# Attention and Fourier-mix feed-forward on one core: the first feed-forward group in its written order, with the last batch's folds and transform moved up

## The chip, the cores and the metric

The kernel runs on one core of a Trainium2 chip. The time is that of one execution on the device, in microseconds (us). Engines are called as in the profile: PE (TensorE, matrix products), PEld (its weight loads), DVE (VectorE), ACT (ScalarE), POOL (GpSimd) and SP (SyncE, which here only issues DMAs). Each works through its own instructions in order, and semaphores make one wait for another.

## What is computed

Attention with a window of 128 and 4 sink tokens, for 4 batches of 768 tokens and 8 heads of 64; then a layer that mixes by a two-dimensional Fourier transform and a feed-forward network with a ReLU, all in 32-bit floats:

```python
keep = is_sink | in_window
scores = np.where(keep, scale * q @ k.T, -1e9)
a = softmax(scores)
x = (a @ v)                                  # 4 x 768 x 512, heads side by side
mixed = np.real(np.fft.fft(np.fft.fft(x, axis=1), axis=2))
u = x + mixed
un = (u - mean(u)) / np.sqrt(var(u) + 1e-6)
out = u + np.maximum(un @ w_ch1, 0.0) @ w_ch2    # 512 -> 2048 -> 512
```

## The kernel before

**Precision.** Each operand of a large product is split into a high part, rounded to PE's fast 32-bit format, and a low part, the difference. A product is then three products: high by high, high by low, low by high. So most tiles have a copy on ACT that makes the high part (L365 `fold_hi`, L402 `z_hi`, L610 and L624 in `convert`) and a subtraction on DVE or POOL that makes the low part (L368 `fold_lo`, L410 `z_lo`, L611, L625).

**Stages.** The attention runs in steps `s`, four to a block of 128 tokens and 24 blocks over all batches. The order of each engine's operations within a step is a hand-written table (`SCHEDULE`), and each operation lags behind the scores by a fixed number of steps. `store_x` (L862) writes a block's result to `u`. A batch's transform (`fourier`, L333) is woven into the steps after it as events: `at(s, engine, fn)` puts a function on a step, and `run_ev` issues it when that step comes. Its parts are

- folds: `fold_n` (L352, sum and difference of block `j` and its mirror block `j + 3`), `fold_m` (L359, L362), `fold_hi`, `fold_lo`, for `j` of 0 to 2. `ready[j]` is the step at which block `j` has been stored, and the folds lie `F_N`, `F_M`, `F_S` steps behind it: 3, 4 or 5, 6 or 7.
- `stage1` (L395): five products (`za` twice, `zr`, `zb` twice), one a step for the last batch, the first of them `S1 = 7` steps behind `ready[2]`. Each has its `z_hi` on ACT and `z_lo` on DVE one step later.
- `stage2a` (L422) and `stage2b` (L443), then `combine` (L448, L449), and `update` (L459, L460), which adds to the rows of `u` and for batches not kept on the chip stores them to DRAM (L462, tile `ud`).

The transform's products take turns on two PSUM banks, and a product waits until the one before it in its bank has been read.

**Feed-forward groups.** The 3072 tokens make six groups of 512. Group 0 (from L1251) takes the hidden layer in 16 turns `f`: `ch1` (L656, 12 matmuls: a block of 128 hidden units), `split` (L1146 ReLU on ACT, L1147 low part on DVE) and `ch2` of the turn before (L1154, 12 matmuls). During these turns the weights arrive. `load_w` fetches a raw block (L584), and `convert(i)` turns it from pairs of 32-bit words into high and low parts, with three DVE passes (L599, L600, L601), a copy on ACT and a subtraction on POOL. Turn `f` converts numbers `2f+4` and `2f+5`; numbers 0 and 1 are events of attention steps 100 and 102, and 2 and 3 stand ahead of turn 0. The blocks of the first matrix go through `w_ring`, whose space the attention's keys held before. For every two of them, `combine_w1` makes sums on POOL (L636 to L639), and a turn later ACT and POOL make high and low parts of these (L643, L644); both are stored to DRAM (L614, L645) for the groups that follow. Block 7 of the second matrix and the later ones go into a pool that is opened when the last batch's transform has finished and its space is free (L1270, L1271).

Events that are left when the attention ends are issued by `do(1)`, one or two steps to a turn, until all are flushed in turn 5.

From turn 6 on (`PREP`), three steps of `prepare(1)` stand at the end of each turn (`PREP_N`). They make the normalized input of group 1: statistics (L515, L516), small operations for the deviations (L522 to L531), normalization (L539), a transposition on PE (L545) with ACT's copy (L1199), sums (L1227 to L1233) and the high and low parts of these (L1237, L1238). Groups 1 to 5 run in a loop of products with the combined weights (L1320) and the second matrix (L1348).

**What sets the order.** Inside `tc.manual_schedule()` each engine's instructions stay in the order in which the program writes them. Outside, the framework's scheduler orders them by its own estimates. In the kernel before, attention steps 0 to 96 (`CUT = 97`) and the loop from L1304 are inside. Steps 97 to 109, and group 0 with the rest of the last transform, are the scheduler's.

Of the kernel before, what the change touches and what calls it, by code (L numbers as in the profile page):

```python
# [11 lines left out]
F32 = mybir.dt.float32  # L12
# [7 lines left out]
P = 128  # L20
# [39 lines left out]
FOLD_AT, FOLD_LAST, FOLD_ENG = (0, 4, 8), (0, 4, 8), "VG"  # L60

F_N, F_M, F_S, ROW = (3, 3), (4, 5), (6, 7), (5, 8, 10)
EV_A = 0

SINK0_AT = 3, 3, "V"
# [71 lines left out]
EV_D, EV_Z = 1, 1  # L137
X_AT, X_NOT = (2,), (81, 97)
SOFT_AT = (0, 1, 2, 3)
S1, S2, UD = 7, 1, 2  # L140
FFT_ORDER = (2, 1, 0)
PARTS = {0: ((2,) * 5, 1, 1), 1: ((2,) * 5, 2, 1), 2: ((2,) * 5, 2, 1)}
PARTS_TAIL = ((1,) * 5, 1, 1)
# [61 lines left out]
def kernel(  # L205
# [17 lines left out]
    def f32(ap):  # L223
        return ap.bitcast(F32)
# [46 lines left out]
    def run(general):  # L271
        tag = "g" if general else ""
        with ExitStack() as p1:
# [8 lines left out]
            def at(s, eng, fn):  # L282
                ev.setdefault((s, eng), []).append(fn)
# [49 lines left out]
            def fourier(b, at, ready):  # L333
# [15 lines left out]
                def fold_n(eng, j, odd):  # L349
                    t = fw.tile([P, DM], F32, tag=f"f{odd}", name=f"f{odd}_{b}_{j}", bufs=2 - odd)  # L350
                    t_["eo", j, odd] = t
                    eng.tensor_tensor(t, u[j], u[NHALF + j], op=ALU.subtract if odd else ALU.add)  # L352

                def fold_m(eng, j, odd):

                    g = t_["eo", j, 0]
                    if odd:
                        t = t_.pop(("eo", j, odd))
                        eng.tensor_tensor(g[:, 257:512], t[:, 1:256], t[:, 511:256:-1], op=ALU.subtract)  # L359
                        t_["g", j] = t_.pop(("eo", j, 0))  # L360
                    else:
                        eng.tensor_tensor(g[:, 1:256], g[:, 1:256], g[:, 511:256:-1], op=ALU.add)  # L362

                def fold_hi(j):
                    A.copy(gh[:, j], t_["g", j])  # L365

                def fold_lo(j):
                    V.tensor_tensor(gl[:, j], t_.pop(("g", j)), f32(gh[:, j]), op=ALU.subtract)  # L368
# [97 lines left out]
                for j in range(NHALF):  # L466
                    k = ready[j]
                    e0, e1 = FOLD_TAIL if tail else FOLD_ENG
                    eng = {"V": V, "G": G}
                    at(k + F_N[0], e0, lambda j=j: fold_n(eng[e0], j, 0))  # L470
                    at(k + F_N[1], e1, lambda j=j: fold_n(eng[e1], j, 1))
                    at(k + F_M[0], e0, lambda j=j: fold_m(eng[e0], j, 0))
                    at(k + F_M[1], e1, lambda j=j: fold_m(eng[e1], j, 1))
                    at(k + F_S[0], "A", lambda j=j: fold_hi(j))
# [155 lines left out]
            def combine_w1(p, pool):  # L630

                t = state.pop(("t", p))
                b11, b21, b12, b22 = t[:, 0, :256], t[:, 0, 256:], t[:, 1, :256], t[:, 1, 256:]
                q = pool.tile([P, 4, 256], F32, tag="tq", name=f"tq{p}")
                o = pool.tile([P, 4, 2, 256], F32R, tag="to", name=f"to{p}")
                G.tensor_tensor(q[:, 1], b12, b11, op=ALU.subtract)  # L636
                G.tensor_tensor(q[:, 0], b22, q[:, 1], op=ALU.subtract)  # L637
                G.tensor_tensor(q[:, 2], b22, b12, op=ALU.subtract)
                G.tensor_tensor(q[:, 3], b21, q[:, 0], op=ALU.subtract)  # L639

                def halves():
# [503 lines left out]
            def split(h, x):  # L1145
                A.activation(h[0], x, AF.Relu)  # L1146
                V.scalar_tensor_tensor(h[1], x, 0.0, f32(h[0]), op0=ALU.max, op1=ALU.subtract)  # L1147
# [100 lines left out]
                        run_ev(s, e)  # L1248
                    s += 1

            po = [ps_o.tile([P, DM], F32, tag=f"o{i}", name=f"o{i}_0") for i in range(len(groups[0]))]  # L1251
            hs = {}
            for i in (2, 3):
                convert(i, wa)
            combine_w1(0, g0)
            for f in range(NF):
                ps = hp.pop(0) if f < 2 else ch1(0, f, unT0)
                hs[f] = [g0.tile([P, 512], F32R, tag=f"h{i}", name=f"h{i}_{f}", bufs=2) for i in range(2)]
                split(hs[f], ps)
                if pw is None:  # L1260
                    do(1)
                if f > 0:
                    ch2(f - 1, hs.pop(f - 1), po)
                for i in range(2 * f + 4, min(2 * f + 6, 2 * NF)):
                    if i % 2 and pw is None:
                        do(1)
                    if W_ORDER[i][0] == 1 and W_ORDER[i][1] == NWA + NHALF and pw is None:
                        while ev:
                            do(1)
                        pf.close()  # L1270
                        pw = p1.enter_context(tc.tile_pool(name="wb" + tag, bufs=1))  # L1271
                        state["x"] = [pw.tile([P, 7, 512], F32R, name=f"x{i}") for i in range(2)]
                        state["xf"] = pw.tile([P, 2, NCC, 256], F32, name="xf")
                    convert(i, wa if pw is None else pw)
                while late:
                    late.pop()()
                if f % 2 == 1 and f // 2 + 1 < NPR:
                    combine_w1(f // 2 + 1, g0)
                if f == PREP:
                    steps = prepare(1)  # L1280
                for _ in range(PREP_N if f >= PREP else 0):
                    next(steps, None)
            for _ in steps:
                pass
            while late:
                late.pop()()

            places = [npool.tile([P, 2, 2, 256], F32R, tag="ld", name=f"w1_c{i}", bufs=LDB) for i in range(LDB)]
            n_all = (len(groups) - 1) * NIT * 7

            def load(n):
                if n < n_all:
                    it, k = divmod(n % (NIT * 7), 7)
                    for j in range(2):
                        nc.sync.dma_start(f32(places[n % NWS][:, j]).rearrange("p s c -> p (s c)"), w_dram[2 * it + j][:, W_PLACE[k]])

            for n in range(LDB):
                load(n)
            ch2(NF - 1, hs.pop(NF - 1), po)
            for i in range(len(po)):  # L1300
                finish(0, i, po[i])
# [187 lines left out]
```

## Time and profile before

| | us |
|---|---|
| Median of three runs (774.32 to 775.8) | 774.68 |
| The profiled execution | 772.87 |
| Its span | 771.1 |
| PE busy | 731.0 |
| DVE busy | 531.6 |
| POOL busy | 291.5 |
| ACT busy | 266.5 |

The granted PE clock was 0.992 on average. The page's second part divides the span into 40 slices of 19.3 us and gives the busy share of each in tenths. In the lists of instructions, columns are start, duration, engine and line, operation, tiles written and read, shapes and count; in brackets stands the idle time of the engine ahead of the instruction and what ended it. In groups, the numbers behind the bar are the busy time and the mean duration in ns, and then the idle time ahead with what ended it. "PE L656" is `ch1`, "PE L1154" `ch2`, "PE L1320" the first product of the loop of groups 1 to 5. Matmuls overlap, so that a unit of 12 shows 2.9 us and the next starts earlier than that.

### The profile page before, as it was taken

The page shows a single profiled execution, that of the slowest core. Times are in us where ns is not written, and L with a number is a line of the kernel's source. Part 1 is how long each engine was busy: PE and PEld are TensorE (multiplying, and loading weights), DVE is VectorE, ACT ScalarE, POOL GpSimd, SP SyncE. Part 2 cuts the span into 40 slices and gives each one's busy share as a digit, 9 for nine tenths or more (in the row PEclk, how much of TensorE's full clock was granted, in tenths as well). Part 3 has the DMA queues.
Part 4 walks back from the last instruction along what each step waited for, and adds up shares of the span by engine and source line. Part 5 has one row for each costly group of instructions (what it writes and reads, how often), then busy time and mean ns, then how long its engine had stood idle before and what let it go on. Part 6 is the DMA issues. An engine that isn't in the chain of part 4 may idle for free.

```text
span 771.1 us, 13868 instructions
## 1 busy us (share of the span) xinstructions
PE 731.0 (95%) x4899; PEld 624.4 (81%) x4899; DVE 531.6 (69%) x1411; ACT 266.5 (35%) x743; POOL 291.5 (38%) x387
## 2 busy tenths in 40 slices
PE   8999998979879898989999999999999999999996
PEld 6676876757668686868989998998998998898895
DVE  6878578899689887867783677467764778342323
ACT  4787666656632324421103111221122110311110
POOL 2567477478779679650015000520034001500000
PEclk9999999999998999999999999999999999999999
DMA  9763525644404678879655756567555655565601
GB/s 307 255 167 114 154 84 169 195 128 139 164 1 191 229 258 282 281 246 378 218 183 180 256 193 191 177 216 254 171 168 189 218 176 183 183 222 170 190 28 60
DMA packets 84446, 145.90 MB, mean 189 GB/s; under 512 B 7532, under 2 KB 32236, under 8 KB 82960
## 3 DMA queue, kind: packets, MB, share of 16 engines
q1 hardware_dynamic: 84080, 141.17, 56.5%
q0 software_dynamic: 288, 3.76, 1.2%
q8 instruction: 41, 0.67, 0.4%
q14 instruction: 37, 0.30, 0.1%
HBM read 120.77 MB, written 24.13 MB: 188 GB/s over the span
## 4 chain that ended last, share of the span: by engine, by line
PE 54%; POOL 2%; DVE 2%; DMA 2%; issue 1%; ACT 1%; SPq 0%; POOLq 0%; DVEq 0%; ACTq 0%
PE o L1348 29%; PE pB L1320 11%; PE pC L1320 7%; PE pA L1320 7%; DMA wd<-to 1%; POOL to L644 1%; DMA w_b<-wd 1%; PE o L1154 0%; DVE u L1159 0%; DVE x L1238 0%; POOL w_ring L611 0%; PE h L656 0%; POOL w L625 0%; POOL tq L639 0%; POOL tq L637 0%
## 5 line engine op out<-in xcount | busy, mean ns | idle before, releaser
L1348 PE MATMUL o<-w,hring 128*128 128x512 f32 x780 | 192.1, 392 | 0.0
L1348 PEld LDWEIGHTS o<-w,hring 128*128 128x128 f32 x780 | 142.4, 188 | 28.2
L1146 ACT ACTIVATE hring<-tmp 128x512 fp32r<-128x512 f32 x60 | 37.9, 632 | 174.8 <-DVE tmp L1393 84.6
L1227 POOL TENSOR_TENSOR s<-xf 128x512 f32<-128x512 f32 x4 | 5.2, 1294 | 240.3 <-DVE xf L1206 240.3
L1147 DVE SCALAR_TENSOR_TENSOR hring<-tmp,hring 128x512 fp32r<-128x512 f32 x60 | 51.8, 863 | 45.6 <-ACT hring L1146 45.6
L1206 DVE STREAM_TRANSPOSE xf<-un 32x128 f32<-32x128 f32 x256 | 77.4, 302 | 3.5
L764 ACT ACTIVATE sm<-sm,mx 128x132 f32<-128x132 f32 x192 | 75.9, 400 | 3.9 <-DVE mx L758 3.9
L1320 PE MATMUL pB<-x,w_b 128*128 128x256 f32 x456 | 59.4, 279 | 0.8 <-DMA w_b<-wd 0.8
L1320 PEld LDWEIGHTS pB<-x,w_b 128*128 128x128 f32 x456 | 56.6, 188 | 1.8 <-issue 1.0
L739 PE MATMUL s<-ring,q 64*128 64x260 f32 x320 | 49.2, 411 | 8.3 <-DVE mx L758 4.3
L758 DVE CUSTOM_DVE_ANT_0 sm<-s,mask 128x132 f32<-128x132 f32 x192 | 48.4, 292 | 8.0 <-PE s L737 3.2
L1147 DVE SCALAR_TENSOR_TENSOR hring<-pA,hring 128x512 fp32r<-128x512 f32 x20 | 13.8, 691 | 57.0 <-ACT hring L1146 57.0
L656 PE MATMUL h<-un_slots,w_ring 128*128 128x512 f32 x192 | 48.6, 400 | 1.5 <-ACT w_ring L610 0.9
L1146 ACT ACTIVATE hring<-pA 128x512 fp32r<-128x512 f32 x20 | 11.9, 596 | 100.2 <-PE pA L1320 100.2
L739 PEld LDWEIGHTS s<-ring,q 64*128 64x128 f32 x320 | 26.8, 185 | 21.0 <-DVE mx L758 5.3
L656 PEld LDWEIGHTS h<-un_slots,w_ring 128*128 128x128 f32 x192 | 35.7, 190 | 9.6 <-ACT w_ring L610 1.3
L1348 PE MATMUL o<-w_gh,hring 128*128 128x512 f32 x120 | 42.5, 395 | 0.0
L834 PE MATMUL xt<-ptl,ldv 128*64 128x128 f32 x384 | 38.8, 285 | 3.1 <-POOL ptl L812 3.1
L1154 PE MATMUL o<-w,h 128*128 128x512 f32 x156 | 39.3, 400 | 1.3 <-POOL w L625 0.8
L1320 PEld LDWEIGHTS pC<-x,w_b 128*128 128x128 f32 x288 | 36.9, 188 | 2.0
L1320 PE MATMUL pA<-x,w_b 128*128 128x256 f32 x288 | 37.5, 279 | 0.5 <-DMA w_b<-wd 0.5
L803 ACT COPY pta<-pt 128x512 f32<-128x512 f32 x48 | 28.1, 584 | 28.5 <-PE pt L796 28.5
(222 smaller groups left out, 1559.6 us busy)
## 6 DMA issues: line engine op xcount, KB each, us to landing
w_b<-wd SPq DMA_DIRECT2D x172, 256.0 KB, 3.5
w_c<-wd SPq DMA_DIRECT2D x108, 256.0 KB, 3.5
raw<-in_moe_w_ch_dram SPq DMA_DIRECT2D x32, 512.0 KB, 4.7
wd<-to SPq DMA_DIRECT2D x8, 1024.0 KB, 6.7
ldv<-in_v_dram SPq DMA_DIRECT2D x28, 256.0 KB, 3.3
ring<-in_qk_dram SPq DMA_DIRECT2D x24, 264.0 KB, 5.0
wd<-w_ring SPq DMA_DIRECT2D x8, 768.0 KB, 3.9
out_dram<-u SPq DMA_DIRECT2D x24, 256.0 KB, 2.5
```

The lines of the kernel that those rows point to most:

```text
L656: T.matmul(ps[:, :tb], a[cc], x[:, :, cc, :], start=n == 0, stop=n == 3 * NCC - 1)
L739: T.matmul(ps[:, j, :P + W], st["q", g][rows, hp, :], keys(g, 2 * hp + j), start=True, stop=True)
L758: V.tensor_tensor_reduce(sm[:, h % 4], ps[:, j, P:P + W], mask[min(qi, 3)], -SCALE, 3.0e38, ALU.add, ALU.min, accum_out=mx[:, 0, h:h + 1])
L764: A.activation(sm[:, h % 4], sm[:, h % 4], AF.Exp, bias=mx[:, 0, h:h + 1], scale=-1.0, accum_out=mx[:, 1, h:h + 1])
L803: A.copy(a, st.pop(("pt", g, hp // 2)))
L834: T.matmul(ps[D * j:D * j + D, p, :], st["v", kb(g) - i][:, h, :], a[:, h % 4, :], start=i == 0, stop=i == n - 1)
L1146: A.activation(h[0], x, AF.Relu)
L1147: V.scalar_tensor_tensor(h[1], x, 0.0, f32(h[0]), op0=ALU.max, op1=ALU.subtract)
L1154: T.matmul(po[i], a[:, ts_], x, start=f == 0 and n == 0, stop=f == NF - 1 and n == 2)
L1206: V.transpose(place[32 * q:32 * q + 32, :, r], un[r].rearrange("p (c q j) -> p c q j", c=NCC, q=4)[:, :, q])
L1320: T.matmul(ps[:, 256 * j:256 * j + 256], w[:, j, a, cs], x[:, xs], start=BANK.index(BANK[k]) == k and j == c == m == 0, stop=j == c == 1 a ...
L1348: T.matmul(po[i], h[:, a, j, ts_], x, start=first and j == m == 0, stop=last and j == 1 and m == 2)
```

## The change

Group 0 goes inside a manual schedule, from the allocation of its accumulators to the closing of its pool, otherwise unchanged and only indented. For the last batch, the folds of its last block lie 1, 2 and 3 steps behind the block instead of 3 to 7, and the first stage of its transform 4 steps behind instead of 7. As all later events of that transform are counted from there, they come three steps earlier.

```diff
+F_LAST = (1, 1), (2, 2), (3, 3)
...
-S1, S2, UD = 7, 1, 2
+S1, S1_LAST, S2, UD = 7, 4, 1, 2
...
                     eng = {"V": V, "G": G}
-                    at(k + F_N[0], e0, lambda j=j: fold_n(eng[e0], j, 0))
-                    at(k + F_N[1], e1, lambda j=j: fold_n(eng[e1], j, 1))
...
-                    at(k + F_S[1], "V", lambda j=j: fold_lo(j))
+                    f_n, f_m, f_s = F_LAST if tail and j == NHALF - 1 else (F_N, F_M, F_S)
+                    at(k + f_n[0], e0, lambda j=j: fold_n(eng[e0], j, 0))
+                    at(k + f_n[1], e1, lambda j=j: fold_n(eng[e1], j, 1))
...
+                    at(k + f_s[1], "V", lambda j=j: fold_lo(j))
...
-                k = ready[2] + S1
+                k = ready[2] + (S1_LAST if tail else S1)
...
-            po = [ps_o.tile([P, DM], F32, tag=f"o{i}", name=f"o{i}_0") for i in range(len(groups[0]))]
-            hs = {}
-            for i in (2, 3):
-                convert(i, wa)
-            combine_w1(0, g0)
-            for f in range(NF):
...
-            pg.close()
+            with tc.manual_schedule():
+                po = [ps_o.tile([P, DM], F32, tag=f"o{i}", name=f"o{i}_0") for i in range(len(groups[0]))]
+                hs = {}
+                for i in (2, 3):
+                    convert(i, wa)
+                combine_w1(0, g0)
+                for f in range(NF):
...
+                pg.close()
```

More of the change, by code (lines that the diff above doesn't have):

```diff
@@ L469, in fourier @@
                     eng = {"V": V, "G": G}
-                    at(k + F_N[0], e0, lambda j=j: fold_n(eng[e0], j, 0))
-                    at(k + F_N[1], e1, lambda j=j: fold_n(eng[e1], j, 1))
-                    at(k + F_M[0], e0, lambda j=j: fold_m(eng[e0], j, 0))
-                    at(k + F_M[1], e1, lambda j=j: fold_m(eng[e1], j, 1))
-                    at(k + F_S[0], "A", lambda j=j: fold_hi(j))
-                    at(k + F_S[1], "V", lambda j=j: fold_lo(j))
+                    f_n, f_m, f_s = F_LAST if tail and j == NHALF - 1 else (F_N, F_M, F_S)
+                    at(k + f_n[0], e0, lambda j=j: fold_n(eng[e0], j, 0))
+                    at(k + f_n[1], e1, lambda j=j: fold_n(eng[e1], j, 1))
+                    at(k + f_m[0], e0, lambda j=j: fold_m(eng[e0], j, 0))
+                    at(k + f_m[1], e1, lambda j=j: fold_m(eng[e1], j, 1))
+                    at(k + f_s[0], "A", lambda j=j: fold_hi(j))
+                    at(k + f_s[1], "V", lambda j=j: fold_lo(j))
                 at(ready[0] + ROW[0], "V", put_row)
@@ L1249, in do @@
                     s += 1
-            po = [ps_o.tile([P, DM], F32, tag=f"o{i}", name=f"o{i}_0") for i in range(len(groups[0]))]
-            hs = {}
-            for i in (2, 3):
-                convert(i, wa)
-            combine_w1(0, g0)
-            for f in range(NF):
[L1257 to L1265, printed above, removed]
+            with tc.manual_schedule():
[5 more added lines that the diff above has]
+                for f in range(NF):
+                    ps = hp.pop(0) if f < 2 else ch1(0, f, unT0)
+                    hs[f] = [g0.tile([P, 512], F32R, tag=f"h{i}", name=f"h{i}_{f}", bufs=2) for i in range(2)]
+                    split(hs[f], ps)
+                    if pw is None:
@@ L1266, in run @@
                         do(1)
-                    if W_ORDER[i][0] == 1 and W_ORDER[i][1] == NWA + NHALF and pw is None:
-                        while ev:
+                    if f > 0:
+                        ch2(f - 1, hs.pop(f - 1), po)
+                    for i in range(2 * f + 4, min(2 * f + 6, 2 * NF)):
+                        if i % 2 and pw is None:
                             do(1)
[L1270 to L1273, printed above, removed]
@@ L1274, in run @@
-                    convert(i, wa if pw is None else pw)
+                        if W_ORDER[i][0] == 1 and W_ORDER[i][1] == NWA + NHALF and pw is None:
+                            while ev:
+                                do(1)
+                            pf.close()
+                            pw = p1.enter_context(tc.tile_pool(name="wb" + tag, bufs=1))
+                            state["x"] = [pw.tile([P, 7, 512], F32R, name=f"x{i}") for i in range(2)]
+                            state["xf"] = pw.tile([P, 2, NCC, 256], F32, name="xf")
@@ L1275, in run @@
+                        convert(i, wa if pw is None else pw)
+                    while late:
+                        late.pop()()
+                    if f % 2 == 1 and f // 2 + 1 < NPR:
+                        combine_w1(f // 2 + 1, g0)
+                    if f == PREP:
+                        steps = prepare(1)
+                    for _ in range(PREP_N if f >= PREP else 0):
+                        next(steps, None)
+                for _ in steps:
+                    pass
                 while late:
@@ L1276, in run @@
                     late.pop()()
[L1277 to L1301, printed above, removed]
@@ L1302, in run, with load @@
-            pg.close()
+                places = [npool.tile([P, 2, 2, 256], F32R, tag="ld", name=f"w1_c{i}", bufs=LDB) for i in range(LDB)]
+                n_all = (len(groups) - 1) * NIT * 7
+                def load(n):
+                    if n < n_all:
+                        it, k = divmod(n % (NIT * 7), 7)
+                        for j in range(2):
+                            nc.sync.dma_start(f32(places[n % NWS][:, j]).rearrange("p s c -> p (s c)"), w_dram[2 * it + j][:, W_PLACE[k]])
@@ L1304, in run @@
+                for n in range(LDB):
+                    load(n)
+                ch2(NF - 1, hs.pop(NF - 1), po)
+                for i in range(len(po)):
+                    finish(0, i, po[i])
+                pg.close()
             with tc.manual_schedule():
```

## The prediction, made before the changed kernel was run

> **What bounds the kernel now.** I read the page first, then the busy times by window, then the engines' instructions in order of time.
>
> ```profile
> span 771.1 us, 13868 instructions
> ...
> PE   8999998979879898989999999999999999999996
> ...
> DVE  6878578899689887867783677467764778342323
> ```
>
> From slice 18 on (347 us) TensorE is full to the end; that is the hand-ordered loop of groups 1 to 5, which the change leaves alone. So the change can only move the time at which that loop begins, and everything below is about that time.
>
> ```profile
> 150.00:160.00 10.00, 10.00 (x102) 7.68 (x98) 9.85 (x36) 7.48 (x31) 7.39 (x13) 1.00 0.37 104
> 160.00:170.00 10.00, 6.67 (x52) 4.75 (x53) 9.69 (x34) 5.72 (x22) 6.57 (x11) 1.00 0.60 194
> ...
> 190.00:200.00 10.00, 10.00 (x88) 8.38 (x86) 8.03 (x32) 6.30 (x24) 5.45 (x10) 1.00 0.41 134
> ```
>
> ```profile
> 230.00:235.00 5.00, 2.45 (x8) 2.43 (x8) 5.00 (x6) 1.39 (x4) 4.92 (x5) 0.50 0.42 179
> ...
> 305.00:310.00 5.00, 5.00 (x17) 3.95 (x16) 5.00 (x6) 2.72 (x5) 3.75 (x3) 0.66 0.99 278
> ```
>
> The columns are the stretch and its length, the busy times of PE, PEld, DVE, ACT and POOL, the granted clock, and the DMA share and rate. In 160 to 170 DVE is full and PE is not: attention waits for DVE there, in 190 to 200 it doesn't. Later PE loses time twice over, to waits and to a lower clock after them.
>
> ```profile
> 207.44 0.43 PE L834 MATMUL xt<-ptl,ldv 128*64 128x128 f32 x2 [3.07 <-POOL ptl L812]
> ...
> 219.89 2.94 PE L656 MATMUL h<-un_slots,w_ring 128*128 128x512 f32 x12
> ...
> 232.55 1.01 PE L395 MATMUL za<-cst,gh 128*128 128x386 f32 x2 [5.43 <-ACT asb L431]
> ...
> 236.50 3.06 PE L1154 MATMUL o<-w,h 128*128 128x512 f32 x12
> ...
> 255.22 0.63 PE L395 MATMUL zb<-cst,gh 128*128 128x386 f32 x2 [2.29 <-DVE zr L407]
> ...
> 282.82 2.92 PE L656 MATMUL h<-un_slots,w_ring 128*128 128x512 f32 x12
> ```
>
> ```profile
> 291.14 2.93 PE L1154 MATMUL o<-w,h 128*128 128x512 f32 x12
> 293.90 2.93 PE L656 MATMUL h<-un_slots,w_ring 128*128 128x512 f32 x12
> 296.67 2.93 PE L1154 MATMUL o<-w,h 128*128 128x512 f32 x12
> ...
> 304.19 0.66 PE L545 MATMUL unt<-ident,un 128*128 128x128 f32 x4 [2.75 <-ACT xf L1199]
> ...
> 344.80 1.58 PE L1320 MATMUL pA<-x,w_c 128*128 128x256 f32 x12
> ```
>
> A unit of 12 matmuls takes 2.77 us (291.14 to 293.90 to 296.67), a turn of the group's loop over f (ch1 and ch2) 5.53. The unit of ch1(7) starts at 282.82 and the loop of group 1 at 344.80. I call 207.44 to 282.82 the first half and the 62.0 us after it the second.
>
> **The change part by part.** The three runs have a median of 774.68 us; the profiled execution took 772.87 (span 771.1), 1.8 less. The sum below is a difference made against the profiled one, and I put it on the median.
>
> *1. Conversions leave the attention.* Where no hand order holds, the scheduler has pulled weight conversions forward:
>
> ```profile
> 154.29 1.17 DVE L599 TENSOR_SCALAR tw<-raw 128x512 int32<-128x512 int32 x1
> ...
> 162.61 0.41 DVE L599 TENSOR_SCALAR tw<-raw 128x512 int32<-128x512 int32 x1
> ```
>
> ```profile
> L599 DVE TENSOR_SCALAR cv<-raw x6: 410/424/1485, 182.2 to 251.3; 128x512 int32<-128x512 int32 x6
> ```
>
> ```profile
> 200.93 5.88 POOL L611 TENSOR_TENSOR w_ring<-tw,w_ring 128x512 fp32r<-128x512 f32 x4
> 206.76 0.63 POOL L812 TENSOR_SCALAR_AFFINE_SELECT ptl<-pta 128x512 f32<-128x512 f32 x1
> ```
>
> Only conversions 0 and 1 are issued in the attention's own steps. In a written group, number 2 and later come behind the attention's hand order. The two at 154.29 and 162.61 stood where DVE was the limit: with two more passes of 0.69 each (rows in step 3) 4.3 us. The `cv` ones from 182.2 on stood where PE was full. I take -3.0 (0 to -4.4), nearer to the row of 160 to 170. On POOL four low passes, 1.47 each, stand ahead of the mask pass for which PE waits 3.07. Two of them go behind it: -2.9. If the scheduler puts other passes in their place, it is anything up to +3.
>
> *2. Folds and transform, first half.* The last fold now follows the last store by one step, not three.
>
> ```profile
> 220.13 0.68 DVE L862 TENSOR_TENSOR us<-x,mx 128x512 f32<-128x512 f32 x1
> ...
> 234.42 1.22 DVE L368 TENSOR_TENSOR gl<-f,gh 128x512 fp32r<-128x512 f32 x1
> ```
>
> ```profile
> L1147 DVE SCALAR_TENSOR_TENSOR h<-h,h 128x512 fp32r<-128x512 f32 x16 | 10.9, 684 | 8.6 <-ACT h L1146 6.8 <-POOL w L625 1.8
> ...
> L352 DVE TENSOR_TENSOR f<-us,us 128x512 f32<-128x512 f32 x6 | 5.6, 956 | 0.1
> ```
>
> From the store to the end of the low half took 15.5 us, and its own five passes and one cast need some 4. The waits of 5.43 and 2.29 go, and with the first the half clock: 232.55 to 236.50 is 3.95 us at a granted 0.50, so 2.0 of it. Together -9.7. Late next is the second transform product. It needs a PSUM bank that the last combine of batch 2 frees, and this is written behind conversions 2 and 3 (0.41 and twice 0.69, 1.8 each) and split 0 with its ReLU (1.3), 5.6 us with itself; the first product covers 1.7: +3.9. The later low halves, written behind conversions: some +2. Net -3.8 (-9.7 if nothing is late next; +3 if DVE's passes there are drawn out as L352's mean is).
>
> *3. Second half.* Bare, PE needs 19 units and four transpositions, 54.1 of its 62.0 us. In the written order DVE has in each turn one split (0.6 to 0.68) and two conversions:
>
> ```profile
> 282.17 0.69 DVE L599 TENSOR_SCALAR cw<-raw 128x512 int32<-128x512 int32 x1
> 282.89 0.69 DVE L600 SCALAR_TENSOR_TENSOR cw<-raw,cw 128x512 int32<-128x512 int32 x1
> 283.62 0.69 DVE L601 SCALAR_TENSOR_TENSOR tw<-raw,cw 128x512 int32<-128x512 int32 x1
> 284.35 0.69 DVE L599 TENSOR_SCALAR cw<-raw 128x512 int32<-128x512 int32 x1
> ```
>
> They start 2.18 apart, so 4.96 of a turn's 5.53 us are taken and 0.57 are spare. Turns 6 to 13 add the preparation of group 1, three steps a turn. The scheduler had spread it out: statistics at 243.76 and the first normalization at 266.85, long before turn 6.
>
> ```profile
> 243.76 0.67 DVE L515 BATCH_NORM_STATS2 bn<-u 128x6 f32<-128x512 f32 x1
> ...
> 266.85 1.47 DVE L539 TENSOR_SCALAR un<-u,stat 128x512 f32<-128x512 f32 x1
> ...
> 311.33 0.54 DVE L539 TENSOR_SCALAR un<-u,stat 128x512 f32<-128x512 f32 x1
> ```
>
> ```profile
> L1238 DVE TENSOR_TENSOR x<-s,x 128x512 fp32r<-128x512 f32 x4 | 3.0, 762 | 0.7 <-ACT x L1237 0.7
> ...
> L527 DVE SCALAR_TENSOR_TENSOR stat<-stat 128x4 f32<-128x4 f32 x4 | 0.7, 164 | 0.1
> ```
>
> Four statistics of 0.67, 14 small ones of 0.16, four normalizations of 0.54, seven low halves of 0.76 and four sums of the same size make 15.5 us. Eight turns spare 4.6, so DVE falls behind PE by 10.9, and PE, which needs every split and every weight, waits for it. Besides, PE meets DVE at the end of turns 9 and 10: a transposition is written after ch2, and its input on DVE after both conversions. PE is there 2.77 us after ch1 ends; DVE after ReLU 0.6, split 0.68, 4.36 and 0.54, 6.2 in all. With the hand-over through ACT's copy, written behind the casts, 3.9 each time and 7.8 for two, in which DVE has no new ch1 to split. Last, the second matrix's block 7 goes into space that the transform gives back only when its six rows are stored:
>
> ```profile
> 276.91 5.14 SPq L462 DMA_DIRECT2D ud<-us  x6
> ```
>
> Written, ReLU 6 stands behind that block's cast on ACT's queue: 5.14 of issues and a landing (3.5, as a load in step 5), less the turn that covers it, 3.1. Sum 21.8: the half becomes 75.9, +13.9. Bounds: DVE alone has 56 us for 10 splits, 16 conversions and the 15.5, so -6 at best; with its passes drawn out +20.
>
> *4. The clock.* The wait of 2.75 at 304.19 was followed by 0.66 over 5 us, 1.7 lost; that of 5.43 by 0.50; that of 3.07 by nothing that I found. Two written waits of about 4 us and more: +2.0 (0 to +4). By the Trainium skill ("TensorE: Matmul & The Clock Gate", "What's actually happening") the array is slowed after an idle window of about 3.4 us and freed after as long a busy one; by that each wait costs an estimated 1.7, which makes this term 3.4. The trace agrees for 5.43, not for 2.75.
>
> *5. Loads of the loop.* Its first weights are written on SP behind the last store of combined weights, which waits for POOL. Before, they had gone out by 341.5.
>
> ```profile
> 338.52 2.97 SPq L1295 DMA_DIRECT2D w_c<-wd  x4
> ```
>
> ```profile
> w_c<-wd SPq DMA_DIRECT2D x108, 256.0 KB, 3.5
> ```
>
> A load lands in 3.5 us, and ch2 of the last turn covers a part: +2.0 (0 to +5).
>
> Sum: -3.0 - 2.9 - 3.8 + 13.9 + 2.0 + 2.0 = +8.2, so 782.9 us. The ends add up to -23 and +35; they won't all meet.
>
> **The rivals.** *Faster, 767:* the gains of 9.7 stand, and the second half grows by no more than some 2 us, because DVE enters turn 6 ahead and the double-buffered h tiles hide its lag. For it: 56 us of DVE work fit into 62. Against it: the meeting in turns 9 and 10 lies in the program's order, not in a margin. It decides if the half stays under 67.7 us; above that, 9.7 is eaten by 4.0 and 5.7. *No change, 774.7:* the written order is near to the scheduler's, so that little moves, or gains and losses meet. PE's order of ch1 and ch2 is the written one already; statistics that ran some 40 us ahead of their written place speak against it. *Much slower, 791:* DVE and POOL hold each other up in the first half, which now holds more of both. L352 took 0.96 on average where passes of its size take 0.69; 0.27 more on 26 conversion passes and six folds is 8.6 us. By the Trainium skill ("SBUF — State Buffer", "Who interferes with whom") a DVE instruction with two SBUF inputs and a POOL instruction that reads SBUF block each other for a whole instruction. L352 agrees with it.
>
> **How the numbers follow.** Forecast 782.9: 0.55. Much slower: 0.15. Faster: 0.22. No change: 0.08. A measurement of this kernel can tell about 0.2% (1.5 us) from no change. So faster 0.22, same 0.08, slower 0.70. The range runs from 769, which leaves out half of the faster case, to 794, which leaves out the end of the much slower one. The forecast's own range is 777 to 789.
>
> **What would show it.** Steps 1 and 2: no L599 between 140 and 195 us, the wait before L834 gone, ch1(0) about 6 us before 219.89, the first `za` product within 5 us of the last fold's low half. Step 3: PE waits of 3 to 6 us before two of the L545 transpositions, waits for L1146 and L1147 in turns 6 to 14, no L515 before turn 6. Step 4: windows under 1.00 behind those waits. Step 5: a DMA wait before the first L1320, which starts near 353. If L1320 starts before 344.8 instead, the forecast is wrong, and step 3 is the place to look.

## The result and the profile after the change

The changed kernel takes 811.21 us (median of 4 runs, 809.96 to 813.16), the kernel before 774.76 on the same chip: a ratio of 1.0471, with a 95% interval of 1.0446 to 1.0495. It is slower by 36.5 us; 8.2 were forecast. The profiled execution took 809.96 us, with a span of 808.1.

The page of the profile after, its span and the rows of TensorE and VectorE:

```profile
span 808.1 us, 13858 instructions
...
PE   7999988989978884878899999999999999999996
...
DVE  6777588797977887585677477846784677443223
```

TensorE now is full from slice 20 on (404 us); before it was from slice 18 on (347 us). TensorE in order of time (start, busy, and in brackets the wait ahead and what ended it):

```profile
201.87 0.43 PE L836 MATMUL xt<-ptl,ldv 128*64 128x128 f32 x2
...
214.40 2.90 PE L658 MATMUL h<-un_slots,w_ring 128*128 128x512 f32 x12
...
224.06 0.62 PE L396 MATMUL za<-cst,gh 128*128 128x386 f32 x2 [2.47 <-ACT asb L432]
...
232.52 0.62 PE L396 MATMUL zb<-cst,gh 128*128 128x386 f32 x2 [2.91 <-DVE za L411]
...
255.67 1.01 PE L444 MATMUL b<-cst,zb 128*128 128x258 f32 x6 [2.76 <-ACT dcs L427]
...
275.00 1.63 PE L444 MATMUL b<-cst,zb 128*128 128x258 f32 x6 [2.93 <-DVE d L450]
...
298.57 2.91 PE L658 MATMUL h<-un_slots,w_ring 128*128 128x512 f32 x12
...
306.35 4.63 PE L1156 MATMUL o<-w,h 128*128 128x512 f32 x10 [4.01 <-DVE h L1149]
314.20 0.66 PE L547 MATMUL unt<-ident,un 128*128 128x128 f32 x4 [3.21 <-DVE un L541]
320.23 1.11 PE L547 MATMUL unt<-ident,un 128*128 128x128 f32 x4 [5.38 <-ACT xf L1201]
321.00 5.03 PE L658 MATMUL h<-un_slots,w_ring 128*128 128x512 f32 x12
...
332.35 1.08 PE L547 MATMUL unt<-ident,un 128*128 128x128 f32 x4 [3.57 <-DVE un L541]
...
380.11 1.69 PE L1323 MATMUL pA<-x,w_c 128*128 128x256 f32 x12 [0.55 <-DMA w_c<-wd]
```

The wait of 3.07 us for POOL (L812 before) is gone, and ch1(0) starts at 214.40 in place of 219.89. The first transform product starts 8.5 us earlier than before, at 224.06. From there on the lead is lost: ch1(7), at 282.82 before, starts at 284.11, and the loop of group 1 at 380.11 in place of 344.80. The turn from 298.57 to 321.00 alone takes 22.4 us where 5.53 is bare.

I cut every profile at three places: ch1(0), ch1(7), and the first product of the loop. Stretch 1 lies between the first two, stretch 2 between the last two. Busy times over both stretches, before:

```profile
219.89:282.82 62.93, 54.47 (x265) 46.19 (x264) 54.07 (x92) 19.66 (x38) 51.59 (x46) 0.95 0.50 181
282.82:344.80 61.98, 56.95 (x245) 45.15 (x244) 50.30 (x74) 25.64 (x45) 44.52 (x41) 0.97 0.79 264
```

and after:

```profile
214.40:284.11 69.71, 58.63 (x265) 49.39 (x264) 55.51 (x77) 18.62 (x37) 43.97 (x42) 0.90 0.49 176
284.11:380.11 96.00, 68.97 (x246) 50.46 (x244) 67.87 (x103) 26.86 (x48) 52.70 (x48) 0.84 0.49 176
```

In stretch 2 PE stands idle for 27.0 us (96.00 less 68.97; 5.0 before) and takes 12.0 longer for the same matmuls, at a granted clock of 0.84. DVE has 17.6 us more to do there. Some 9 of them are statistics, small operations for the deviations and a normalisation that the scheduler had placed in stretch 1; most of the rest is the same passes taking longer (the four low halves of sums, L1238 before, take 5.7 us in place of 3.0). All the same DVE stands idle for 28.1 of the 96.0 us. Of PE's 27.0, 12.2 are waits ahead of transpositions (3.21, 5.38 and 3.57) and 12.5 waits for a turn's ReLU or its low part (L1148, L1149). From the loop's first product to the end it is 428.0 us (426.3 before). Together -5.5 for ch1(0), +6.8, +34.0 and +1.7: 37.0, the difference of the spans.

### The profile page after: what moved, and what is told of

Same layout as the page of the kernel before. It is cut to its first block, busy times and chain, and to the rows that moved or that the text cites. A ratio compares the mean times of both kernels' runs of the same rounds, so it can differ in the third digit from the quotient of the medians.

```text
span 808.1 us, 13858 instructions
## 1 busy us (share of the span) xinstructions
PE 745.7 (92%) x4899; PEld 632.1 (78%) x4899; DVE 542.1 (67%) x1411; ACT 265.8 (33%) x743; POOL 286.8 (35%) x387
## 4 chain that ended last, share of the span: by engine, by line
PE 68%; DVE 20%; ACT 4%; issue 3%; POOL 2%; DMA 2%; SPq 0%; ACTq 0%; DVEq 0%; POOLq 0%
PE o L1351 27%; PE pB L1323 10%; PE pA L1323 7%; PE pC L1323 7%; PE xt L836 4%; PE s L741 3%; PE pt L798 2%; DVE tw L603 1%; DVE cw L602 1%; DVE cw L601 1%; DVE sm L760 1%; DVE cv L603 1%; PE za L396 1%; PE zb L396 1%; PE h L658 1%
## 5 line engine op out<-in xcount | busy, mean ns | idle before, releaser
L1148 ACT ACTIVATE hring<-tmp 128x512 fp32r<-128x512 f32 x60 | 37.9, 632 | 174.5 <-DVE tmp L1396 84.3
L1149 DVE SCALAR_TENSOR_TENSOR hring<-tmp,hring 128x512 fp32r<-128x512 f32 x60 | 51.9, 864 | 45.3 <-ACT hring L1148 45.3
L766 ACT ACTIVATE sm<-sm,mx 128x132 f32<-128x132 f32 x192 | 75.9, 400 | 3.8 <-DVE mx L760 3.7
L658 PE MATMUL h<-un_slots,w_ring 128*128 128x512 f32 x192 | 55.1, 441 | 1.7 <-POOL w_ring L613 1.4
L1156 PE MATMUL o<-w,h 128*128 128x512 f32 x156 | 45.9, 446 | 11.5 <-DVE h L1149 7.8
L1149 DVE SCALAR_TENSOR_TENSOR hring<-pA,hring 128x512 fp32r<-128x512 f32 x20 | 13.8, 692 | 59.8 <-ACT hring L1148 59.8
L658 PEld LDWEIGHTS h<-un_slots,w_ring 128*128 128x128 f32 x192 | 41.0, 219 | 12.3 <-POOL w_ring L613 2.3
L1156 PEld LDWEIGHTS o<-w,h 128*128 128x128 f32 x156 | 33.1, 217 | 22.0 <-DVE h L1149 10.0
L1148 ACT ACTIVATE hring<-pA 128x512 fp32r<-128x512 f32 x20 | 12.0, 598 | 103.0 <-PE pA L1323 103.0
L1323 PEld LDWEIGHTS pA<-x,w_b 128*128 128x128 f32 x288 | 37.3, 193 | 3.5 <-issue 2.4
```

The lines of the kernel that those rows point to most:

```text
L658: T.matmul(ps[:, :tb], a[cc], x[:, :, cc, :], start=n == 0, stop=n == 3 * NCC - 1)
L766: A.activation(sm[:, h % 4], sm[:, h % 4], AF.Exp, bias=mx[:, 0, h:h + 1], scale=-1.0, accum_out=mx[:, 1, h:h + 1])
L1156: T.matmul(po[i], a[:, ts_], x, start=f == 0 and n == 0, stop=f == NF - 1 and n == 2)
L1323: T.matmul(ps[:, 256 * j:256 * j + 256], w[:, j, a, cs], x[:, xs], start=BANK.index(BANK[k]) == k and j == c == m == 0, stop=j == c == 1 a ...
```

## The experiments

Each run was timed beside the kernel before, whose median was 773.22 to 776.29 us in these pairs; the ratios go by the pair. Theory A: the loss is the written place of group 1's preparation in turns 6 to 13. It splits later into A1 (transpositions that meet normalisations written right ahead of them) and A2 (more DVE work than the turns hold). Rival B: the order of casts and ReLUs in each turn. C: the earlier folds. D: block 7's cast, which waits for the row stores. E: the lower clock.

**Each part alone.** `e1_order_only` undoes the second part:

```
-F_LAST = (1, 1), (2, 2), (3, 3)
+F_LAST = F_N, F_M, F_S
-S1, S1_LAST, S2, UD = 7, 4, 1, 2
+S1, S1_LAST, S2, UD = 7, 7, 1, 2
```

> The changed kernel with its second part undone: the last block's folds 3 to 7 steps behind it again and the first stage of the last transform 7 again; group 0 stays in the written order. If the loss lies in the written order (theory A, and the rival B that puts it on the turns' own order), this kernel stays close to the changed one: 808 to 816 us, a few us more if the earlier folds had gained something. If the early folds are the loss (rival C: they crowd DVE and ACT beside the attention and the first turns), it falls to 785 us or less.

812.87 us, ratio to before 1.0503 (1.0485 to 1.0520). The loss is in the written order; within it the earlier folds (C) are not a cause.

`e2_folds_only` is the kernel before with `F_LAST` and `S1_LAST` and no written order.

> The kernel before with the second part alone: last folds 1 to 3 steps behind their blocks, first stage of the last transform 4, group 0 still in the scheduler's order. Theory A and rival B: 768 to 776 us, that is between a gain of 6 us and no change, because the last row of the transform waits for these folds (5.43 us before the first product of the last transform in the trace of before). Rival C: 785 us or more.

781.13 us, 1.0076 (1.0054 to 1.0099). This is a miss: alone, the folds cost some 6 us. The profiled execution, the longest of the four with 783.31 us, starts ch1(0) at 223.84, 4.0 later than before, and its stretch 1 is 5.7 longer:

```profile
223.84:292.46 68.62, 58.52 (x266) 49.91 (x265) 63.15 (x93) 19.53 (x38) 51.84 (x46) 0.88 0.46 169
```

DVE is busy for 63.15 of its 68.62 us, 9 more than before. That the earlier folds make the scheduler pack DVE more tightly is only argued.

**Without the preparation.** `e3_no_prep`:

```
+                            for t in state["x"]:
+                                G.memset(f32(t), 0.25)
+                            G.memset(state["xf"], 0.25)
...
-                        steps = prepare(1)
+                        steps = iter(())
```

> The changed kernel without the preparation of group 1 inside group 0: no statistics, deviations, normalisations, transpositions, sums or splits in turns 6 to 13; the operands of group 1's products are filled by three memsets on POOL in turn 5 instead, so its results are not the reference's. Theory A (the written place of the preparation is what costs: 17 to 18 us of DVE work and four meetings of PE with DVE, and PE's lower clock behind them): the stretch from the eighth first-matrix product to the loop falls from 96 us to 60 to 68 and the time to 775 to 785 us. Rival B (the order of conversions, casts, ReLUs and remainders in each turn costs it without the preparation): the stretch stays above 80 us and the time above 795 us.

This kernel leaves the preparation out and fills its results with a constant. 789.60 us, 1.0201 (1.0167 to 1.0234), and stretch 2 is 75.4 us, between the forecasts of A and of B. Of these, 7.8 are the run's own, in a line of TensorE, because the memsets hold POOL:

```profile
301.92 4.63 PE L658 MATMUL h<-un_slots,w_ring 128*128 128x512 f32 x10 [7.80 <-POOL w_ring L613]
```

A holds the larger part: 20.6 us of stretch 2 go, and some 28 if that wait is taken off as well. PE's waits for ReLUs and low parts there fall from 12.5 us to 2.8.

**The written order for turns 0 to 5 only.** `e4_hand_first`:

```
                if f == 5:
                    hand.close()
```

> The changed kernel with the written order for turns 0 to 5 only; from turn 6 the scheduler orders again. It lifts the statistics, deviations and the first normalisation ahead of turn 3, puts the ReLU of turn 6 ahead of the cast that waits for the row stores, and spreads the transpositions. Theory A: the second stretch is again as before the change, 62 to 68 us instead of 96, and the time 776 to 784 us. Rival B, if the coupling sits in the turns as such and not in the preparation: most of the loss stays, 795 us or more. Rival D (the wait of turn 6's ReLU behind that cast is the main loss, 6 to 9 us, and the rest follows from it): also about 780 to 800 us, told from A by the run without the preparation, which keeps that wait.

784.41 us, 1.0130 (1.0100 to 1.0161). Both come out just above A's forecast. Stretch 2 is 68.8 us; stretch 1 became 72.8. The scheduler has lifted statistics and deviations into it (231 to 242 us); that they are what makes it longer is argued here.

**Where in the preparation.** `e5_spread` replaces three steps a turn by a plan, with a second buffer for the normalised block:

```
plan = {6: [(st, 0), (st, 1), (st, 2)], 7: [(st, 3), (dv, 8)], 8: [(dv, 9), (mk, 0)], 9: [(tn, 0), (mk, 1)],
        10: [(tn, 1), (mk, 2)], 11: [(tn, 2), (mk, 3)], 12: [(tn, 3), (sums_, 0), (put, 2)],
        13: [(put, 0), (put, 1)], 14: [(put, 3), (put, 4), (put, 5)], 15: [(put, 6)]}
```

> The changed kernel with the preparation of group 1 written in other places: each block is normalised a turn before its transposition (blocks 0 to 3 normalised at the end of turns 8 to 11, into two buffers in place of one, transposed at the end of turns 9 to 12), and the sums and splits of the operands stand in turns 12 to 15 in place of 11 to 13. All its DVE work stays in turns 6 to 15. Theory A1 (the loss is the meetings: a transposition queued on PE right behind a normalisation that stands last in DVE's queue, and the lower clock behind those waits; the trace after the change has 6.8 us of waits for normalisations, 5.4 for the copy between two of them, and 4.0 for the first remainder behind them): 788 to 797 us. Theory A2 (the loss is DVE's load: with two conversions a turn, 4.4 us, a split 0.8 and the preparation it has more than PE's 5.4 to 5.9 us a turn, wherever the transpositions stand): 803 us or more.

796.71 us, 1.0271 (1.0235 to 1.0307). TensorE in turns 9 and 10 of this run:

```profile
314.98 1.11 PE L547 MATMUL unt<-ident,unx 128*128 128x128 f32 x4 [4.25 <-DVE unx L1297]
315.75 4.37 PE L658 MATMUL h<-un_slots,w_ring 128*128 128x512 f32 x12
319.96 2.93 PE L1156 MATMUL o<-w,h 128*128 128x512 f32 x12
322.72 0.60 PE L547 MATMUL unt<-ident,unx 128*128 128x128 f32 x4
323.07 3.02 PE L658 MATMUL h<-un_slots,w_ring 128*128 128x512 f32 x12
...
329.14 3.01 PE L658 MATMUL h<-un_slots,w_ring 128*128 128x512 f32 x12
```

The first transposition still waits, behind the statistics and deviations; the second and third don't, and the turn from 323.07 to 329.14 is again 6.1 us. DVE's busy time in stretch 2 is unchanged (67.81), yet the stretch is 8.8 us shorter. That is A1: the waits ahead of transpositions fall from 12.2 us to 4.7. Those for ReLUs and low parts don't fall (15.9, from 12.5).

`e6_sums_pool` takes DVE work away instead:

```
-                    start, put = sums(1, V)
+                    start, put = sums(1, G)
```

> The changed kernel with the four sums and seven subtractions of group 1's operands (turns 11 to 13) on POOL instead of DVE: 10 to 12 us of DVE work in the trace after the change less, at the same places. Theory A2: 6 us or more off, 799 to 805 us. Theory A1: 808 to 812 us, since the waits at turns 9 and 10 lie before these sums; POOL's own instructions of 1.1 to 1.5 us could delay the remainders of the blocks by a few us in turns 12 and 13.

812.69 us, 1.0474 (1.0445 to 1.0504).

```profile
282.66:383.63 100.97, 65.31 (x246) 50.45 (x244) 57.74 (x96) 26.76 (x48) 64.96 (x62) 0.81 0.49 175
```

DVE has 10.1 us less to do (57.74) and stretch 2 is longer. But the run has a long wait of its own. The sums now come from POOL, behind its other passes, ACT's copies of them (L1239) stand ahead of the ReLU, and PE waits for that:

```profile
372.18 0.62 ACT L1239 CAST x<-s 128x512 fp32r<-128x512 f32 x1 [6.13 <-POOL s L1235]
...
373.87 7.38 PE L1156 MATMUL o<-w,h 128*128 128x512 f32 x24 [10.53 <-ACT h L1148]
```

The longest such wait after the change is 2.22. So this run doesn't settle A2: this wait stands against whatever the lighter DVE gained.

**Block 7's cast.** `e7_cast_late` keeps its cast and remainder and issues them behind the next split:

```
+                if f == NWA + NHALF:
+                    state["cast"] = parts
...
                     split(hs[f], ps)
+                    state.pop("cast", lambda: None)()
```

> The changed kernel with the cast and the remainder of the block that opens the second pool (its second-matrix block 7) issued behind the ReLU of turn 6 instead of ahead of it; the ReLU no longer stands behind a cast that waited 8.6 us for the row stores. Theory D (that wait shifts everything behind it): 803 to 806 us. Theory A: the DVE queue of turns 6 to 13 is the limit from there on and takes the gain back, 807 to 811 us.

808.21 us, 1.0424 (1.0397 to 1.0451). This is 3 to 4 us by the medians and the ratios (1.9 between the two spans, 806.2 and 808.1), about what the prediction gave this wait. The time lies in the range given for A, not in D's: more than half of a wait of 8.6 us is taken back further on. ScalarE's lines after the change show the wait that goes:

```profile
286.98 0.62 ACT L626 CAST w<-cv 128x512 fp32r<-128x512 f32 x1 [8.58 <-DMA ud<-us]
287.50 0.59 ACT L1148 ACTIVATE h<-h 128x512 fp32r<-128x512 f32 x1
```

`e8_three` joins the last three edits.

> The three edits together: transpositions a turn behind their normalisations, sums on POOL, the late cast. Theories A1 and A2 both: 780 to 792 us, as the run without any preparation gave 789.6 with about 9 us of a wait of its own. If neither holds, and the loss is in the turns' own order, it stays above 798 us.

797.37 us, 1.0277 (1.0252 to 1.0301): no better than the transpositions alone. With the sums on POOL, the copies of the operands hold ACT in the last turns here too, and TensorE waits once 9.2 us for a ReLU behind them. A miss.

**Preparation earlier, ReLU first, and both.** `e9_prep_early` is the plan with statistics in turns 0 to 3, deviations in 4 and 5, everything else two turns earlier and the operands' splits a turn behind their sums. `e10_relu_first` applies the edit of `e7_cast_late` to the second conversion of every turn (`if f % 2 and i > 3`). `e11_both` has both.

> The changed kernel with the preparation written earlier and looser: one block's statistics at the end of each of turns 0 to 3, the deviations in turns 4 and 5, normalisations in turns 6 to 9 with each transposition a turn behind, the sums in turn 11 and the splits, each at least a turn behind the sum it reads, in turns 12 to 14. The version with only the transpositions a turn behind gave 796.7 us and still waited 3.7 and 4.2 us behind the statistics and deviations in turns 6 to 8, and 1.4 to 2.1 us five times in turns 13 to 15. Theory A (the preparation's places): 779 to 787 us, less what the early statistics cost the transform. Rival B (casts and ReLUs in each turn): the gain stops at 790 us or more.

> The changed kernel with the second conversion's cast and remainder of each turn issued behind the next turn's ReLU instead of ahead of it; nothing else moved. In the trace after the change the remainder of a split waits 2.2 us for ACT in turns 1, 3 and 5, where ACT's ReLU stands behind two casts and a store's casts that wait for DVE, and two transform rows wait behind them. Rival B: 6 to 10 us of turns 1 to 5 and some of the later turns come back, 797 to 804 us. Theory A with theory D: only the 3 us of the late cast, 806 to 809 us.

> Both edits, the preparation in its earlier places and each second cast behind the next ReLU. If A and B each hold a part, the sum: 768 to 780 us. If the ReLU's place is not a cause of its own, as with the preparation's places alone, 779 to 787 us.

793.97 us, 1.0266 (1.0249 to 1.0283); 803.18, 1.0390 (1.0355 to 1.0426); 786.90, 1.0160 (1.0132 to 1.0187). The two gains add up: 2.05 and 0.81 points of the ratio apart, 3.11 together. The first and the third time missed the ranges given for A and for both; 786.90 lies even in the range for a ReLU that is no cause, and only beside the 793.97 does it show one. The early places shorten stretch 2 to 79.5 us, but gained hardly more than the spread ones in all: TensorE now waits 3.9 us for DVE in front of a row of the transform, and the profiled execution, the longest of its five (798.47), starts ch1(0) only at 219.77. The second edit also moves block 7's cast, yet in its profile stretch 2 is only 1.0 us shorter than after the change and stretch 1 4.8: B is a cause of its own in stretch 1. ScalarE in turns 2 and 3, after the change:

```profile
249.91 0.62 ACT L612 CAST w_ring<-tw 128x512 fp32r<-128x512 f32 x1 [3.80 <-DVE tw L603]
253.22 0.62 ACT L612 CAST w_ring<-tw 128x512 fp32r<-128x512 f32 x1 [2.68 <-DVE tw L603]
253.74 1.13 ACT L645 CAST to<-tq 128x512 fp32r<-128x512 f32 x2
254.78 0.59 ACT L1148 ACTIVATE h<-h 128x512 fp32r<-128x512 f32 x1
255.27 0.35 ACT L427 COPY dcs<-dc 1x257 f32<-1x257 f32 x1
```

and with the ReLU first:

```profile
250.99 0.62 ACT L617 CAST w_ring<-tw 128x512 fp32r<-128x512 f32 x1 [3.28 <-DVE tw L603]
251.52 1.14 ACT L659 CAST to<-tq 128x512 fp32r<-128x512 f32 x2
252.56 0.59 ACT L1162 ACTIVATE h<-h 128x512 fp32r<-128x512 f32 x1
253.77 0.62 ACT L617 CAST w_ring<-tw 128x512 fp32r<-128x512 f32 x1 [0.62 <-DVE tw L603]
254.30 0.36 ACT L427 COPY dcs<-dc 1x257 f32<-1x257 f32 x1
```

In the first, the ReLU and the transform's copy stand behind a cast that waits 2.68 us for DVE, and DVE then waits for that ReLU before it can split; the row at 255.67 waits 2.76 us for the copy. In the second, the ReLU comes 2.2 us earlier and the row doesn't wait. Stretch 1 falls to 64.9 us; it was 67.0 to 69.7 in six profiles in which its order is the one after the change.

**The clock.** `e12_warm` puts products whose results are overwritten ahead of six waits:

```
+                    if f in KEEP:
+                        pre["n"] = banks[1][0].tile([P, 512], F32, tag="n", name=f"warm_{f}", bufs=1)
+                        warm(pre["n"], KEEP[f])
```

> The changed kernel with products of no use (128x512, results overwritten) on TensorE ahead of six of its waits in turns 9, 10, 14 and 15: 12, 12, 20, 12, 8 and 8 of them, as many as fit in the wait at full clock. Nothing else is moved. The trace after the change has about 10 us of units made longer by a clock of 0.67 to 0.83 in that stretch. Theory E (the clock is a cause by itself): 801 to 805 us, with those units at their full-clock times. Theory A (PE meets DVE again a turn later, so that faster units only lengthen the next wait): 808 to 812 us, with the same units short and the waits behind them longer.

807.93 us, 1.0452 (1.0433 to 1.0470), an interval that overlaps with that of the change. TensorE around turn 9:

```profile
299.17 2.91 PE L659 MATMUL h<-un_slots,w_ring 128*128 128x512 f32 x12
...
320.89 0.66 PE L548 MATMUL unt<-ident,un 128*128 128x128 f32 x4 [0.82 <-ACT xf L1214]
321.30 3.00 PE L659 MATMUL h<-un_slots,w_ring 128*128 128x512 f32 x12
```

```profile
283.48:376.94 93.46, 77.15 (x318) 59.01 (x316) 69.81 (x105) 26.78 (x48) 54.01 (x49) 0.96 0.52 185
```

The clock is back at 0.96, the unit of 5.03 us takes 3.00, and the turn from 299.17 to 321.30 takes 22.1 us where it took 22.4. The six groups hold 72 products; at 0.23 us each (2.77 by 12) they take 16.6 of the 77.15 us. So PE's own matmuls take an estimated 60.5 us, 8.4 less than after the change, and stretch 2 is 2.5 us shorter. E holds for little: a faster unit mostly reaches the next wait sooner.

**What is left.** `e13_dev_thin` is `e11_both` with statistics in turns 0 and 1 and the deviations three at a time over turns 2 to 6. `e15_no_folds` is that with the second part of the change undone. `e16_hand_relu` is `e4_hand_first` with the ReLU first.

> The last version with both edits, and the deviations spread thinner: statistics in turns 0 and 1, then three of the fourteen small deviation instructions at the end of each of turns 2 to 5 and the rest in turn 6. In the version with both edits the deviations stood as two lumps of 3.5 to 4 us on DVE (instructions of 0.17 us that became 0.66 to 1.25 us while POOL worked), and a transform row waited 4.3 us and the first normalisation 3.1 us behind them. Theory A: 780 to 784 us. If the lumps only fill time in which DVE would have waited anyway: 785 to 789 us.

> The version with the thin deviations, and the second part of the change undone (folds 3 to 7 steps behind, first stage of the last transform 7). In the written order the folds gained 1.7 us, in the scheduler's they cost 6.7. If what they cost lies at the end of the attention and in the scheduler's placing of conversions there, this version is 1 to 4 us slower than the one with them; rival C, that they cost in any order: 5 us or more faster.

> The written order for turns 0 to 5 with each second cast behind the next ReLU, the scheduler from turn 6 on. The same split without the casts' move gave 784.4 us, 72.8 us from the first product of group 0 to its eighth and 68.8 from there to the loop. Theories A and B together: the first stretch falls by 5 to 8 us as in the run with the casts alone, 775 to 779 us, level with the kernel before. If the statistics that the scheduler lifts into turns 0 to 3 are what the first stretch loses by, it stays at 781 us or more.

790.07 us, 1.0183 (1.0164 to 1.0201): thinner deviations gain nothing. 789.68, 1.0177 (1.0158 to 1.0197): in the fully written order the folds cost and gain nothing. 775.64 (10 runs), 1.0012 (0.9989 to 1.0035): level with the kernel before, as forecast. Stretch 1 is 67.1 us there and stretch 2 63.6. Of TensorE's waits in that run one was long:

```profile
PE zb L396 <- DVE za L411: 5.3, 1, 5.3
```

The last two runs take that version further: `e17_hand_stats` writes a statistic at the end of each of turns 2 to 5, and `e18_hand_nofold` undoes the folds.

> The version with turns 0 to 5 written (each second cast behind the next ReLU) and the scheduler from turn 6 on, with one change: the statistics of group 1's blocks stand in the written part too, one at the end of each of turns 2 to 5, so that the scheduler cannot lift them and the deviations into turns 0 and 1, where the first reversed product of the transform waited 5.3 us for DVE behind them. If what is lifted there is what the first stretch loses: 3 to 5 us off in that stretch, 770 to 773 us, faster than both kernels. If the deviations then miss in the second stretch: 775 to 779 us.

> The same version, with turns 0 to 5 written and the scheduler from turn 6 on, and the second part of the change undone (folds 3 to 7 steps behind, first stage of the last transform 7). In the fully written order the folds cost nothing that could be measured (790.1 with, 789.7 without). The same here: 774 to 778 us.

780.57 us, 1.0077 (1.0049 to 1.0105): stretch 1 falls to 64.9 us, by 2.2 where 3 to 5 were expected, and the wait above to 2.6, but stretch 2 rises to 72.2. That the lifted work is missing there is argued: DVE has 60.87 us to do in it, where it had 52.78. 780.55, 1.0078 (1.0050 to 1.0105): without the early folds TensorE waits for the last block's halves,

```profile
PE za L396 <- ACT gh L366: 7.3, 1, 7.3
PE za L396 <- DVE gl L369: 5.8, 1, 5.8
```

and the folds gain about 5 us by the ratios. In `e15_no_folds` two such waits stood as well (6.9 and 3.5) and cost nothing in all; that there something else was late too is argued. Both runs missed their forecasts. No version beat the kernel before.

## Why the prediction was wrong, step by step

*Step 1* held: -5.9 forecast, -5.5 measured. The block stored at 197.15 us before is stored at 194.72: 2.4 for the two conversions that left the attention (3.0 forecast). The other 3.1 are the POOL wait of 3.07 (2.9 forecast); two low passes stand ahead of the mask in place of four. One reading in it failed. Conversions 2 and 3 did not come behind the attention: their passes still run from 179.76 and 187.85 us.

*Step 2*, -3.8 forecast, came out at +6.8. The wait of 2.29 went, that of 5.43 fell to 2.47, and the half clock behind it went. The 3.9 for the second product did not come: conversions 2 and 3, with which it was worked out, were done, the last combine of batch 2 ran at 224.83, and the second product followed the first without a wait. The part that failed is "the later low halves, written behind conversions: some +2". One low half cost 2.91 and two rows of the transform 2.76 and 2.93, 8.6 in all. With the clock behind them PE's matmuls in stretch 1 took 4.2 us longer than before (58.63, 54.47), where the sum had 2.0 less. I had looked at DVE's order and not at ACT's, where each ReLU and each transform copy stands behind the casts of the conversions before it. The 2.91 is such a case, a transform copy behind a cast:

```profile
230.88 0.62 ACT L612 CAST w_ring<-tw 128x512 fp32r<-128x512 f32 x1 [4.26 <-DVE tw L603]
231.40 0.47 ACT L403 CAST za<-za 128x386 fp32r<-128x386 f32 x1
```

With the ReLU first, 2.1 to 4.8 us came back: the wait of 2.76 went, the other two stayed. Of the rest, 2.0 over the stretch of before, I have no cause shown.

*Step 3* had the right mechanism, PE waiting for the written preparation and conversions, and the wrong size: 75.9 us forecast, 96.0 measured. Over the bare 54.1 these are 27.0 of idle time, where its terms made 21.8, and 14.9 by which the matmuls took longer than bare. Among the waits the meetings are the term that was too small: two of 3.9 forecast, 12.2 measured. Turn 9 holds two transpositions and one buffer for the normalised block, so PE waits for a normalisation (3.21) and then for ACT's copy, behind the casts (5.38); in turn 10 it waits once more (3.57). The plan that loosens them and moves the sums took off some 15 us of the whole, 8.8 of them in stretch 2; turns 9 and 10 alone are 11.5 us shorter in its profile (298.57 to 333.08 before it, 300.03 to 323.07 with it). The DVE excess, 10.9 forecast, stands beside 12.5 of waits for ReLUs and low parts, of which 2.8 are left without the preparation. Whether this is the amount of DVE's work or its place the runs don't tell apart, as `e6_sums_pool` brought a wait of its own. Block 7's cast, 3.1 forecast, measured 3 to 4.

*Step 4*, +2.0 forecast, looks far too small beside the 12.0 us by which PE's matmuls grew in stretch 2 over the kernel before. But the run that kept the clock gained 1.5 us by the ratios, 3.3 by the medians, so as a term that adds to the waits 2.0 was about right. Most of the 12.0 is waiting time under another name: with its own matmuls at an estimated 60.5 us, PE spends the other 33 us of that run's stretch 2 waiting or in fillers. At nearly full clock (0.96), then, the waits that step 3 sized at 21.8 are an estimated 33.

*Step 5* had the size (+2.0 forecast, +1.7 measured) but not the place. The wait for the first weights is 0.55 and lies ahead of the loop's first product. The 1.7 lie behind that product, where PE waits 2.23 us ahead of the fourth unit (386.86) and runs the next two slowly; what ended that wait the profile doesn't show. That the numbers agree is in part luck.

So the sign and the kind of mechanism held, and the size failed: in step 3 by 20 us, as its waits were sized too small, the meetings above all, and in step 2 by 11, part of it ACT's queue. Of the rivals, "faster" rested on DVE having slack, "no change" on the two orders being alike, and "much slower" (791) on DVE and POOL holding each other up in stretch 1; none priced what happened. What remains unexplained is the 12 us between the best fully written version (786.9) and the kernel before: in its profile stretch 1 is 7.6 and stretch 2 10.1 us longer, and ch1(0) starts 5.8 earlier.

## What to carry to other kernels

When a written order replaces a scheduler's, list what the scheduler had lifted out of that stretch, and give every product that one engine makes for another a full turn before it is read, with a buffer of its own; two hand-overs in one turn and a third in the next cost 12.2 us here, where a count of instructions had given 7.8 for two. On each in-order queue put the instruction that another engine needs next (here the ReLU) ahead of those that themselves wait for another engine. Write by hand only the part where you can place everything better: with turns 0 to 5 written, the ReLU first, and the rest left to the scheduler the loss was gone.

## What the runs showed of the hardware

Small DVE instructions stretch to the end of POOL's. DVE after the change, in turn 8:

```profile
302.48 0.64 DVE L526 TENSOR_SCALAR stat<-stat 128x4 int32<-128x4 int32 x1
303.16 0.17 DVE L529 SCALAR_TENSOR_TENSOR stat<-stat 128x4 f32<-128x4 f32 x1
303.36 0.58 DVE L531 TENSOR_TENSOR stat<-stat 128x4 f32<-128x4 f32 x1
303.97 0.65 DVE L533 SCALAR_TENSOR_TENSOR stat<-stat 128x4 f32<-128x4 f32 x1
```

and POOL at the same time:

```profile
302.37 0.72 POOL L638 TENSOR_TENSOR tq<-tw 128x256 f32<-128x256 f32 x1
303.17 0.74 POOL L639 TENSOR_TENSOR tq<-tw,tq 128x256 f32<-128x256 f32 x1
303.87 0.72 POOL L640 TENSOR_TENSOR tq<-tw 128x256 f32<-128x256 f32 x1
```

An instruction of 0.17 us takes 0.58 to 0.65 when POOL is already in one of its own (the one at 303.16, which starts first, isn't held), and ends within 0.04 us of it: 303.12 and 303.09, 303.94 and 303.91, 304.62 and 304.59. The page "SBUF — State Buffer" of the Trainium skill, "Who interferes with whom", says that the engine that issues first gets the shared port pair for its whole instruction and the other is blocked; these lines agree. I had priced the fourteen of them at 0.16 each, 2.2 us; they took 5.6.

The granted clock fell behind waits of 2.91 (0.83 over 230 to 240 us), 2.76 (0.86 over 250 to 260) and 2.93 (0.71 over 270 to 280), and not behind 2.47 (1.00 over 220 to 230). Before the change it didn't fall behind 3.07 either (1.00 over 205 to 215), so the length of a wait alone doesn't decide. The Trainium skill ("TensorE: Matmul & The Clock Gate", "What's actually happening") has an idle window of about 3.4 us; here 2.76 was enough.
